# Six loads at a time, reciprocals over DRAM and whole visits in the opening of a fused attention and MLP kernel

## The chip, the cores and the metric

One core of one Trainium2 chip. Times are device microseconds of a whole execution; a ratio is taken only against runs of the kernel before in the same rounds on the same chip, because the kernel before alone reads 379 to 391 us from chip to chip and round to round. Ratios and their intervals are of fast runs alone; the medians are of all runs. With one core at work a run is called slow by its time alone, when it lies over 1.5% above the fastest run of the same kernel, so a ratio of a few runs leans on the fastest one. Pairs and visits are counted from 0: the fifth visit is V(5).

## The reference, cut to what matters

```python
# B, H, S, D = 8, 8, 576, 64; factor = 4
out_d     = softmax(q_d @ k_d.T / 8) @ v_d      # q, k, v averaged over 4 tokens
out_local = softmax(q @ k.T / 8 where |i-j| < 4) @ v
x         = (repeat(out_d, 4) + out_local)      # -> 4608 tokens x 512
h         = x @ w_in                            # 512 x 2048
out       = (h * sigmoid(h)) @ w_out            # 2048 x 512
```

## The kernel before

Attention works on 32 pairs of heads. Each pair has these units: T (transposes Q and K on TensorE), S (scores), Z (the softmax sums), PV (output), and, for the first eight pairs, VP (the averaged V by matmul). The MLP has 144 first-layer groups of 4 matmuls and 36 x 4 second-layer groups of 4. A small planner in the kernel orders all units on each engine; the order is then fixed. Up to pair 9 the units stand one by one (the prologue); from there a *visit* V(n) holds PV of pair n-2, Z of pair n-1, S of pair n and T of pair n+1 in one block, and MLP groups stand between visits.

The sums have to be inverted and spread over 64 partitions. For the first eight pairs TensorE does that, from three bf16 parts of the reciprocal; for all others the reciprocals are written to DRAM and read back as a broadcast:

```python
def after_Z(p):
    one("DVE", f"r{p}", 1.2, lambda e: e.reciprocal(zr[i], CD[:, :, 360:432]), ...)
    if p < NDIR:                       # NDIR = 8: parts for TensorE
        ... rh (ACT), rx, rm, rl (DVE)
        return
    dma("ACT", f"z{p}", scr[u], zf, ...)                # 72 KB to DRAM
    for h in range(2):
        dma("ACT", f"b{p}", Rb[u][half(h)], src, ...)   # 2 x 180 KB back, broadcast

def RB(p):                             # 18 matmuls into AB, then ACT copies AB to Rb
    ...

def after_PV(p):                       # DVE: xo = CD * Rb, then POOL adds into xT
    ...

        T(0)
        for n in range(10):
            T(n + 1); S(n)
            if n > 0: Z(n - 1)
            if n > 1: PV(n - 2)
            if 0 < n <= NDIR:
                RB(n - 1); VP(n - 1)
            if n > 4: G1((2, 4, 4, 4, 2)[n - 5])
        for n in range(10, 46):
            V(n); ...                  # with 4 first-layer and 4 second-layer groups
```

(Cut: constants, loads, casts, the planner.) CD, two of the eight PSUM banks, takes the sums of one pair and the output of another; pairs 1 and 3 use HP instead, which the MLP's first layer needs as well. Loads of Q, K and V are issued by SP, weights by POOL.

The softmax here doesn't subtract the row's maximum and nothing guards it: scores larger than these inputs give would overflow.

## Time and profile before

The median is 382.89 us of three runs (379.94 to 384.25); in the rounds with the changed kernel 383.57 of four. The profiled execution has a span of 378.6 us. Two stretches tell it: up to the tenth visit, and the rest (columns: length, busy us and count of TensorE, weight loads, DVE, ACT and POOL, granted clock, DMA share, GB/s).

```profile
0.00:92.17 92.17, 61.00 (x1505) 46.44 (x1506) 62.13 (x119) 45.46 (x91) 60.62 (x96) 0.98 1.04 249
92.17:378.60 286.43, 277.05 (x3842) 174.81 (x3872) 175.60 (x260) 131.43 (x229) 108.01 (x119) 0.99 0.52 145
```

TensorE idles 31.2 of 92.2 us in the prologue and 9.4 of 286.4 us afterwards. So most of what can be won lies in the prologue.

### The profile page before, as it was taken

The numbers are of one execution on the slowest core, as the hardware profiler recorded it, in microseconds if no ns is written. First come the engines' busy times: TensorE is split into PE (matmuls) and PEld (weight loads), VectorE is DVE, ScalarE is ACT, GpSimd is POOL, SyncE is SP. The second block draws the span as 40 slices with busy tenths as digits, with TensorE's granted clock in tenths as the row PEclk, the third lists the DMA queues.
The fourth block names the chain that finished last, engine by engine and source line by source line (L and its number), as shares of the span: only waits on it lengthen the run. The fifth ranks groups of instructions, "written<-read, shape, count | busy, mean of one in ns | idle before, by whom it ended". The sixth has DMA issues, their size and how long they took to land.

```text
span 378.6 us, 12323 instructions
## 1 busy us (share of the span) xinstructions
PE 338.1 (89%) x5346; PEld 221.3 (58%) x5376; DVE 237.7 (63%) x379; ACT 176.9 (47%) x320; POOL 168.6 (45%) x215
## 2 busy tenths in 40 slices
PE   2475689886999989989999999999999999999996
PEld 1364576654566656656665666666656566666642
DVE  6555468698677858877787776778875434434310
ACT  3635356554355535545544545555543343443421
POOL 6849568367455736665655566555221100000000
PEclk9999999899999999999999999999999999999999
DMA  7999999958978896887887887522222211001012
GB/s 211 280 290 308 244 275 244 237 161 232 257 174 245 220 271 164 222 242 212 223 219 214 213 225 214 162 96 79 84 77 79 66 39 44 28 31 54 28 57 83
DMA packets 77823, 64.37 MB, mean 170 GB/s; under 512 B 47050, under 2 KB 59850, under 8 KB 77770
## 3 DMA queue, kind: packets, MB, share of 16 engines
q1 hardware_dynamic: 66250, 46.68, 45.3%
q10 hardware_dynamic: 7296, 10.62, 10.4%
q0 software_dynamic: 4224, 6.29, 7.7%
q8 instruction: 42, 0.69, 0.8%
q14 instruction: 11, 0.09, 0.1%
HBM read 54.46 MB, written 11.21 MB: 173 GB/s over the span
## 4 chain that ended last, share of the span: by engine, by line
PE 77%; DMA 8%; DVE 4%; SPq 4%; issue 4%; ACT 2%; ACTq 1%; POOL 0%; POOLq 0%
PE HP L339 35%; PE o L339 22%; PE pe_ L339 7%; DMA scr<-zr 6%; PE CD L339 6%; PE AB L339 4%; SPq L426 4%; DMA qk<-in_k_dram 2%; PE o L531 1%; ACTq L426 1%; PE pe_ L531 1%; DVE Pt L586 1%; DVE gT L773 1%; DVE xo L728 1%; DVE gT L699 1%
## 5 line engine op out<-in xcount | busy, mean ns | idle before, releaser
L339 PE MATMUL HP<-xT,w_in_sb 128*128 128x512 f32 x576 | 164.1, 421 | 2.4 <-DVE gT L773 2.4
L773 DVE SCALAR_TENSOR_TENSOR gT<-th,HP 128x512 bf16<-128x512 f32 x144 | 96.4, 683 | 96.9 <-ACT th L771 96.9
L771 ACT ACTIVATE th<-HP 128x512 f32<-128x512 f32 x144 | 85.8, 598 | 84.1 <-PE HP L339 80.5
L339 PEld LDWEIGHTS HP<-xT,w_in_sb 128*128 128x128 f32 x576 | 106.8, 191 | 29.6 <-DVE gT L773 3.1
L339 PE MATMUL o<-w_out_bf,gT 128*128 128x512 bf16 x437 | 102.0, 380 | 1.8
L339 PEld LDWEIGHTS o<-w_out_bf,gT 128*128 128x128 bf16 x464 | 42.1, 98 | 56.1 <-issue 5.7
L755 POOL TENSOR_TENSOR xT<-xo 128x576 fp32r<-128x576 f32 (+3 forms) x48 | 44.4, 938 | 62.7 <-DVE xo L728 62.7
L513 POOL CAST vb<-vs 128x640 bf16<-128x640 f32 x30 | 21.5, 717 | 60.6 <-PE CD L339 52.5
L788 ACT ACTIVATE osb<-o 128x512 f32<-128x512 f32 x29 | 17.3, 597 | 60.9 <-PE o L339 49.7
L690 DVE RECIPROCAL zr<-CD 128x144 f32<-128x144 f32 x30 | 31.7, 1056 | 9.9 <-PE CD L339 5.2
L503 POOL CAST qkb<-qk 128x1152 bf16<-128x1152 f32 x30 | 34.6, 1154 | 3.6 <-PE pe_ L531 2.9
L518 POOL TENSOR_TENSOR vt<-vq 128x512 f32<-128x512 f32 x24 | 30.6, 1274 | 0.2 <-POOL vd L520 0.2
L728 DVE TENSOR_TENSOR xo<-CD,Rb 128x720 f32<-128x720 f32 x30 | 26.8, 895 | 0.0
L339 PE MATMUL pe_<-w_out_bf,gT 128*128 128x512 bf16 x109 | 26.1, 380 | 0.2
L531 PE MATMUL o<-idn,qkb 64*64 64x64 bf16 x576 | 17.6, 206 | 8.8 <-DVE qkb L498 5.6
L545 DVE TENSOR_REDUCE kd<-kT 128x144 bf16<-128x576 bf16 x32 | 23.6, 737 | 0.7 <-ACT kT L541 0.6
L541 ACT ACTIVATE kT<-pe_ 128x576 bf16<-128x576 bf16 x32 | 20.9, 652 | 6.7 <-PE pe_ L531 6.2
L582 ACT ACTIVATE Pt<-AB 128x576 bf16<-128x576 f32 x32 | 20.7, 647 | 6.1 <-PE AB L339 3.8
L531 PEld LDWEIGHTS o<-idn,qkb 64*64 64x64 bf16 x576 | 14.2, 119 | 11.7 <-DVE qkb L498 6.5
L531 PE MATMUL pe_<-idn,qkb 64*64 64x64 bf16 x576 | 17.1, 206 | 1.3 <-DVE qkb L500 0.7
L339 PE MATMUL CD<-Pd,vd 64*64 64x72 bf16 x360 | 15.1, 210 | 3.3 <-DVE xo L728 3.0
L339 PEld LDWEIGHTS pe_<-w_out_bf,gT 128*128 128x128 bf16 x112 | 10.0, 98 | 13.6 <-issue 3.2
(78 smaller groups left out, 350.9 us busy)
## 6 DMA issues: line engine op xcount, KB each, us to landing
vs<-in_v_dram SPq DMA_DIRECT2D x126, 80.0 KB, 4.1
qk<-in_q_dram SPq DMA_DIRECT2D x32, 288.0 KB, 4.9
out_dram<-osb SPq DMA_DIRECT2D x36, 256.0 KB, 2.1
qk<-in_k_dram SPq DMA_DIRECT2D x31, 288.0 KB, 5.7
Rb<-scr ACTq DMA_DIRECT2D x48, 180.0 KB, 4.7
vq<-in_v_dram SPq DMA_DIRECT2D x24, 256.0 KB, 5.9
w_in_sb<-in_moe_w_in_dram POOLq DMA_DIRECT2D x4, 1024.0 KB, 9.9
w_out_bf<-in_moe_w_out_dram POOLq DMA_DIRECT2D x4, 512.0 KB, 8.2
```

The lines of the kernel that those rows point to most:

```text
L339: L.op(u, lambda t: t.matmul(out_, lhsT, rhs, start=start, stop=stop, skip_group_check=True), r, w)
L503: one("POOL", f"c{p}", 1.15, lambda g: g.tensor_copy(qkb[j][:, :, :], qk[i][:, :, :]), r=[R(f"qk{i}0"), R(f"qk{i}1")], w=[R(f"qkb{j}0"), R ...
L513: one("POOL", f"cw{p}", 0.72, lambda g: g.tensor_copy(vb[m][:, :, :], vs[i][:, :, :]), r=rr, w=[R(f"vb{m}")])
L518: one("POOL", f"va{p}", 1.3, lambda g: g.tensor_tensor(vt[:, :, :], vq[i][:, :, 0:128], vq[i][:, :, 128:256], ALU.add), r=rr, w=[R("vt")])
L531: L.op(u, lambda e, o=o, w=w, j=j: e.transpose(o, w, idn[half(j), :]), [R("id"), R(f"qkb{n}{x}")], [rE if x else rF])
L541: one("ACT", f"ek{p}", 0.68, lambda e: e.activation(kT[j][:, 3:579].rearrange("p (g r) -> p g r", r=9), pe_[:, 0:288].bitcast(BF16).rearra ...
L545: one("DVE", f"mk{p}", 0.74, lambda e: e.tensor_reduce(kd[j][:, 0:SD], kT[j][:, 3:579].rearrange("p (g r) -> p g r", r=4), AX.X, ALU.add), ...
L690: one("DVE", f"r{p}", 1.2, lambda e: e.reciprocal(zr[i][:, :, :], CD[:, :, 360:432]), r=rCD, w=[R(f"zr{i}")], prio=-4)
L728: one("DVE", f"m{p}", 0.92, lambda e: e.tensor_tensor(xo[x][:, :, :].rearrange("p x (m n) -> p x m n", n=72), CD[:, :, 0:360].rearrange("p ...
L755: one("POOL", f"a{p}", 0.15 + n * 0.0019, lambda g, dst=dst, in0=in0, in1=in1: g.tensor_tensor(dst, in0, in1, ALU.add), r=[R(f"xo{x}")], w ...
L771: one("ACT", f"t{j}_{f}", 0.62, lambda e: e.activation(th[tb][:, :], hps[hb], AF.Tanh, scale=0.5), r=[rH[hb]], w=[R(f"th{tb}")], prio=-1)
L773: one("DVE", f"s{j}_{f}", 0.71, lambda e: e.scalar_tensor_tensor(gT[j % 2][:, f, :], th[tb][:, :], 1.0, hps[hb], ALU.add, ALU.mult), r=[rH ...
```

## The change

Its intent: hold the loads of later pairs back so that the next pair's arrive soon; take the broadcasts off TensorE in favour of a round trip over DRAM (except pair 3); and use whole visits from V(5) on. Weights are also asked for later, priorities are strengthened, and the query sums of pairs 4 to 7 go from POOL to DVE.

```diff
-NDIR = 8
+DIRECT = (3,)
+NFLOW = 6
@@ a load takes one of six tokens, and waits for the landing of the load that had it @@
+            if flow:
+                x = R(f"flow{nflow[0] % NFLOW}")
+                nflow[0] += 1
+                r, w = list(r) + [x], list(w) + [x]
@@ after_T @@
-            if p >= NVP:
+            if p >= 4:
                 one("DVE", f"mq{p}", ...)
@@ after_Z @@
-            if p < NDIR:
+            if p in DIRECT:
@@ weights @@
-        for c, t in enumerate((10, 14, 18, 22, 34, 38, 42, 46)):
+        for c, t in enumerate((16, 23, 29, 35, 41, 46, 51, 56)):
             load_w(c).ready = float(t)
@@ the prologue @@
-        for n in range(10):
+        for n in range(5):
             T(n + 1); S(n); Z(n - 1); VP(n - 1); PV(n - 2)      # shortened
-                RB(n - 1)
+        RB(3)
+        PV(3)
+        G1(3)
+        V(5)
+        G1(3)
+        for n, m in zip(range(6, 10), (3, 3, 2, 2)):
+            VP(n - 2)
+            V(n)
+            G1(m)
```

(Cut: priorities, the issue of the first K loads from ACT, the rule that a pair's V is not asked for before its Q and K, and the main loop, whose contents stay.)

More of the change, by code (lines that the diff above doesn't have):

```diff
@@ L167, in __init__ @@
         self.units = []
+        self.boost = 0
     def unit(self, eng, name, cost, prio=None, dcost=0.0):
@@ L172, in unit @@
         if u.prio is None:
-            u.prio = u.idx
+            u.prio = u.idx - self.boost
         self.units.append(u)
@@ L421, in constants, with dma @@
                     base=-64 * j, pattern=[[-1, 5], [0, 64]], channel_multiplier=1), r=selr, w=selr)
-        def dma(eng, name, out_, in_, w, sem, dcost, r=(), prio=None, cost=0.42):
+        nflow = [0]
+        def dma(eng, name, out_, in_, w, sem, dcost, r=(), prio=None, cost=0.42, flow=False):
+            if flow:
+                x = R(f"flow{nflow[0] % NFLOW}")
+                nflow[0] += 1
+                r, w = list(r) + [x], list(w) + [x]
             return one(eng, name, cost, lambda s: s.dma_start(out_, in_), r, w, sem, prio, dcost)
@@ L429, in load_qk @@
             i = p % NQK
+            ek = "ACT" if p < 2 else "SP"
             if p == 0:
-                dma("SP", "lkx", Rb[NR - 1][64:128, 0:576], bass.AP(tensor=k.tensor, offset=k.offset,
+                dma("ACT", "lkx", Rb[NR - 1][64:128, 0:576], bass.AP(tensor=k.tensor, offset=k.offset,
                                                                    ap=[[576, 64], [1, 576]]),
-                    [R(f"Rb{NR - 1}1")], "kx", 0.5, prio=-20)
+                    [R(f"Rb{NR - 1}1")], "kx", 0.5, prio=-20, flow=True)
             dma("SP", f"lq{p}", qk[i][:, 0, :], bass.AP(tensor=q.tensor, offset=q.offset + 128 * p * 576,
                                                         ap=[[576, 128], [1, 576]]),
-                [R(f"qk{i}0")], f"qk{i}0", 0.85, prio=10 * p)
+                [R(f"qk{i}0")], f"qk{i}0", 0.85, prio=10 * p, flow=True)
             n = 128 if p < NPAIR - 1 else 64
-            dma("SP", f"lk{p}", qk[i][0:n, 1, :], bass.AP(tensor=k.tensor, offset=k.offset + (128 * p + 64) * 576,
+            dma(ek, f"lk{p}", qk[i][0:n, 1, :], bass.AP(tensor=k.tensor, offset=k.offset + (128 * p + 64) * 576,
                                                           ap=[[576, n], [1, 576]]),
-                [R(f"qk{i}1")], f"qk{i}1", 0.85, prio=10 * p)
+                [R(f"qk{i}1")], f"qk{i}1", 0.85, prio=10 * p, flow=True)
         def load_v(p):
@@ L462, in load_v @@
                                   ap=[[64, 64], [58 * 64, hi - lo], [1, 64]])
-                    dma("SP", f"lv{p}", d[:, lo:hi, :], win, w, f"vs{i}{h}{j}", 0.46, prio=10 * p + 15)
+                    dma("SP", f"lv{p}", d[:, lo:hi, :], win, w, f"vs{i}{h}{j}", 0.46, prio=10 * p + 15, flow=True)
         def load_vq(p):
@@ L471, in load_vq @@
                 bass.AP(tensor=t, offset=o, ap=[[256, 128], [S_ * D_, 2], [1, 256]]),
-                [R(f"vqm{i}")], f"vq{i}", 1.0, prio=10 * p + 21)
+                [R(f"vqm{i}")], f"vq{i}", 1.0, prio=10 * p + 21, flow=True)
             for j in range(2):
@@ L475, in load_vq @@
                     bass.AP(tensor=t, offset=o + 128 * 256, ap=[[256, 16], [S_ * D_, 2], [1, 256]]),
-                    [R(f"vqe{i}{j}")], f"vqe{i}{j}", 0.12, r=[R(f"vqc{i}1"), R(f"vqc{i}3")], prio=10 * p + 21)
+                    [R(f"vqe{i}{j}")], f"vqe{i}{j}", 0.12, r=[R(f"vqc{i}1"), R(f"vqc{i}3")], prio=10 * p + 21, flow=True)
         def load_w(c):
@@ L690, in after_Z @@
             one("DVE", f"r{p}", 1.2, lambda e: e.reciprocal(zr[i][:, :, :], CD[:, :, 360:432]),
-                r=rCD, w=[R(f"zr{i}")], prio=-4)
+                r=rCD, w=[R(f"zr{i}")], prio=-400000)
             zf = zr[i][:, :, :].rearrange("p x n -> p (x n)")
-            if p < NDIR:
+            if p in DIRECT:
                 h, m, l = rpart
-                one("ACT", f"rh{p}", 0.25, lambda e: e.activation(h, zf, AF.Copy), r=[R(f"zr{i}")], w=[rpr[0]], prio=-4)
+                one("ACT", f"rh{p}", 0.25, lambda e: e.activation(h, zf, AF.Copy), r=[R(f"zr{i}")], w=[rpr[0]], prio=-400000)
                 one("DVE", f"rx{p}", 0.22, lambda e: e.tensor_tensor(rrest, zf, h, ALU.subtract),
-                    r=[R(f"zr{i}"), rpr[0]], w=[R("g1_5")], prio=-4)
-                one("DVE", f"rm{p}", 0.16, lambda e: e.tensor_copy(m, rrest), r=[R("g1_5")], w=[rpr[1]], prio=-4)
+                    r=[R(f"zr{i}"), rpr[0]], w=[R("g1_5")], prio=-400000)
+                one("DVE", f"rm{p}", 0.16, lambda e: e.tensor_copy(m, rrest), r=[R("g1_5")], w=[rpr[1]], prio=-400000)
                 one("DVE", f"rl{p}", 0.22, lambda e: e.tensor_tensor(l, rrest, m, ALU.subtract),
-                    r=[R("g1_5"), rpr[1]], w=[rpr[2]], prio=-4)
+                    r=[R("g1_5"), rpr[1]], w=[rpr[2]], prio=-400000)
                 return
             eng = "ACT"
-            dma(eng, f"z{p}", scr[u][:, :], zf, [R(f"scr{u}")], f"scr{u}", 0.2, r=[R(f"zr{i}")], prio=-5)
+            dma(eng, f"z{p}", scr[u][:, :], zf, [R(f"scr{u}")], f"scr{u}", 0.2, r=[R(f"zr{i}")], prio=-500000)
             for h in range(2):
@@ L706, in after_Z @@
                 dma(eng, f"b{p}", Rb[u][half(h), :], src, [R(f"Rb{u}{h}")], f"Rb{u}{h}", 0.85,
-                    r=[R(f"scr{u}")], prio=-5)
+                    r=[R(f"scr{u}")], prio=-500000)
         def RB(p):
@@ L755, in after_PV @@
                 one("POOL", f"a{p}", 0.15 + n * 0.0019, lambda g, dst=dst, in0=in0, in1=in1: g.tensor_tensor(
-                    dst, in0, in1, ALU.add), r=[R(f"xo{x}")], w=xblk(kc, t + a, t + e_), prio=-2)
+                    dst, in0, in1, ALU.add), r=[R(f"xo{x}")], w=xblk(kc, t + a, t + e_), prio=-200000)
         ng1 = [0]
@@ L824, in V @@
         def V(n):
-            pv = n - 2 if n - 2 < NPAIR else None
+            pv = n - 2 if n - 2 < NPAIR and ("PV", n - 2) not in made else None
             z = n - 1 if n - 1 < NPAIR else None
@@ L860, in feed @@
                         continue
+                    if name in ("lv", "lvq") and ("lqk", p) not in made:
+                        continue
                     made.add((name, p))
@@ L866, in bass_hourglass_attn__then__act_silu_kernel @@
         feed()
-        for c, t in enumerate((10, 14, 18, 22, 34, 38, 42, 46)):
+        for c, t in enumerate((16, 23, 29, 35, 41, 46, 51, 56)):
             load_w(c).ready = float(t)
         todo = [(j, f) for j in range(NSUP) for f in range(16)]
+        todo2 = [(j, tt) for j in range(NSUP) for tt in range(4)]
         def G1(n):
@@ L874, in G1, with G2 @@
                     g1(*todo.pop(0))
+        def G2(parts):
+            j, tt = todo2[0]
+            u = 4 * j + tt
+            bank, rb = (o0, rF) if u < 22 or u % 2 else (pe_, rE)
+            for p in parts:
+                g2(j, tt, p, bank, rb)
+            if parts[-1] == 3:
+                todo2.pop(0)
+        L.boost = 100000
         T(0)
         feed()
-        for n in range(10):
+        for n in range(5):
             T(n + 1)
@@ L883, in bass_hourglass_attn__then__act_silu_kernel @@
                 Z(n - 1)
+                VP(n - 1)
             if n > 1:
@@ L886, in bass_hourglass_attn__then__act_silu_kernel @@
                 feed()
-            if 0 < n <= NDIR:
-                RB(n - 1)
-                VP(n - 1)
-            if n > 4:
-                G1((2, 4, 4, 4, 2)[n - 5])
-        for n in range(10, 46):
+        RB(3)
+        PV(3)
+        feed()
+        G1(3)
+        V(5)
+        feed()
+        G1(3)
+        for n, m in zip(range(6, 10), (3, 3, 2, 2)):
+            L.boost = 100000 if n < 8 else 0
+            VP(n - 2)
+            V(n)
+            feed()
+            G1(m)
+        L.boost = 0
+        n = 10
+        while todo or todo2:
             if n < NPAIR + 2:
@@ L895, in bass_hourglass_attn__then__act_silu_kernel @@
                 feed()
-            j, tt = divmod(n - 10, 4)
-            bank, rb = (o0, rF) if n < NPAIR or n % 2 else (pe_, rE)
-            G1(1)
-            g2(j, tt, 0, bank, rb)
-            G1(1)
-            g2(j, tt, 1, bank, rb)
-            G1(1)
-            g2(j, tt, 2, bank, rb)
-            g2(j, tt, 3, bank, rb)
-            G1(1)
+            m = 4
+            G1(1 if m else 0)
+            G2((0,))
+            G1(1 if m else 0)
+            G2((1,))
+            G1(1 if m else 0)
+            G2((2, 3))
+            G1(m - 3 if m else 0)
+            n += 1
         P = Prog()
```

## The prediction

> **What bounds the kernel now.** I read the busy table first, then five stretches of time that I cut where the kernel changes character, then the waits of the first 92 us, then the chain that ended last around the end of that stretch.
>
> ```profile
> span 378.6 us, 12323 instructions
> PE 338.1 (89%) x5346; PEld 221.3 (58%) x5376; DVE 237.7 (63%) x379; ACT 176.9 (47%) x320; POOL 168.6 (45%) x215
> ```
>
> TensorE is the bound on average, but that average hides two kernels in one. The stretches (columns: busy us and count of PE, weight loads, DVE, ACT, POOL, then granted clock, DMA share, GB/s):
>
> ```profile
> 0.00:20.00 20.00, 7.04 (x242) 5.63 (x243) 12.17 (x45) 9.44 (x17) 14.20 (x43) 1.00 0.89 248
> 20.00:55.00 35.00, 23.45 (x646) 19.36 (x644) 19.87 (x29) 15.69 (x34) 22.10 (x28) 1.00 1.23 275
> 55.00:92.00 37.00, 30.51 (x623) 21.43 (x620) 29.98 (x47) 20.33 (x40) 24.32 (x26) 0.95 0.93 224
> 92.00:300.00 208.00, 202.04 (x3510) 130.96 (x3535) 151.63 (x226) 102.93 (x182) 108.01 (x119) 0.99 0.67 183
> 300.00:379.00 79.00, 75.02 (x333) 43.86 (x337) 24.08 (x35) 28.50 (x48) 0.00 (x0) 1.00 0.12 44
> ```
>
> From 92 us on TensorE is 97% busy (202.04 of 208) and 95% at the end; nothing there can be won without removing matmuls. Before 92 us it is busy 7.04 + 23.45 + 30.51 = 61.0 us and idle 31.0 us. That prologue is pairs 0 to 9 of attention plus the first 16 of 144 first-layer groups of the MLP, and 16 of them is also what the changed prologue holds. At 92.17 us the tenth visit starts, the first that is followed by second-layer matmuls. From there to the end the kernel takes 378.6 - 92.2 = 286.4 us.
>
> What fills the prologue's holes, from its waits and its groups:
>
> ```profile
> ACT Rb L718 <- PE AB L339: 14.5, 8, 4.7
> POOL vb L513 <- DMA vs<-in_v_dram: 8.1, 3, 3.3
> ```
>
> ```profile
> L339 PE MATMUL AB<-gT 128*128 128x144 bf16 (+1 forms) x144 | 13.1, 260 | 3.2 <-DVE gT L699 3.1
> L718 ACT ACTIVATE Rb<-AB 128x720 f32<-128x720 f32 x8 | 6.2, 771 | 14.5 <-PE AB L339 14.5
> ```
>
> The first pair: the broadcast of the reciprocals on TensorE (18 matmuls a pair, 144 in all) costs 13.1 us of TensorE, and it sits in the one in-order stream behind a split of the reciprocal in three bf16 parts on DVE and ACT. The second: the cast of V on POOL stands 8.1 us in three waits for loads. The loads behind them take a median of 8.7 us, 12.3 at most, between 15 and 40 us (17 V loads), where 275 GB/s move at a DMA share of 1.23; the first loads of the kernel land after 3 to 4 us.
>
> **What the Trainium skill says.** "DMA: Bandwidth & Descriptors", section "Queues, rings and completion order": each DMA engine goes round the queue rows that have work, packet by packet, and the SP and the ACT issuer each own a row. So fewer loads under way on SP do not lift total bandwidth; they shorten the line that a load stands in, and a transfer issued from ACT never stood in that line, it only shares the engines. The trace agrees as far as it goes: loads got slow as soon as the weight row was active. The same page, "Anatomy of one DMA", gives a fixed part of about 2 us a transfer, which is why a round trip over DRAM of two transfers cannot be short; here the trace has 2.6 to 5.2 us for the write of the reciprocals and 3.8 to 6.9 (median 5.2) for the broadcast read. "TensorE: Matmul & The Clock Gate", section "Part 1: The HAM clock gate", has half clock after some 3.4 us of idleness; the trace shows the same 18 broadcast matmuls in 1.98 us before 50 us and 0.96 us after 60, so a prologue with holes pays twice.
>
> **The change part by part.** The visits' contents after pair 9 are the same, so I ask when the tenth visit can start.
>
> Removed: seven of eight broadcasts. TensorE loses 7/8 of 13.1 = 11.5 us (some 1 us each late, 2 early), ACT 7 x 0.77 = 5.4 us, and 7 x 0.32 for the first part; DVE loses 7 x (0.37 + 0.60 + 0.70) = 11.7 us, in a prologue where DVE was 9.7 us busy of the 10 between 80 and 90. DVE gets back four query sums from POOL, 4 x 0.74 = 3.0 us.
>
> Added: seven round trips over DRAM. Each is reciprocal 1.06, issue about 0.4, landing 3 to 4.5, two issues 1.1, landing 4.7 to 7, multiply 0.90, handoffs 0.5: 12 to 15 us, with the visit's own 1.4 us. In DMA: 72 KB written and read again as 2 x 180 KB, 0.43 MB a pair, 3.0 MB in all; at 275 GB/s that is 11 us of DMA time. The accumulator banks couple it to TensorE: from the fifth visit on visit n+2 may not write before the multiply of visit n's reciprocals, because both live in the same PSUM banks. So two interleaved chains, odd and even visits, each step 12 to 15 us long, that is a visit every 6 to 7.5 us. The matmul work of such a visit is 1.3 (visit) + 0.9 (V sums) + 2 x 0.9 (two first-layer groups) = 4 us, so the round trip, not TensorE, sets the pace there.
>
> The start, worked through the changed order of instructions with durations of the trace. Until 12 us nothing changes: the first scores wait for constants on POOL (the before trace has them at 11.5). Then the second pair's scores come forward, the third pair's come at about 19.5 instead of 22.3, because no broadcast stands before them (2 us) and its V load is not behind six others. The first pair's reciprocal is ready at 17.3, written by 21 to 22, broadcast by 27 to 29, multiplied by 29. The third Z needs that bank, so it stands at 29 to 30 (before: 29.3; nothing won yet). Then scores of pair 4, PV of pair 2, V sums, about 34; the multiply of pair 1 (its broadcast is behind ACT's evacuations, 35 to 36) frees the other bank; Z, PV and the one remaining broadcast of pair 3 end at about 41; the multiply of pair 2 lands at 43 to 45. The fifth visit starts at about 44. (Before, the comparable work, S5 and Z4, was at 47 to 51.)
>
> From there: visit 7 at 44 + 12 to 15 = 56 to 59, visit 9 at 68 to 74. The even chain starts later, since the first two first-layer groups need the first four pairs multiplied and added (47.5) and are in front: visit 6 at 50.5, visit 8 at 62.5 to 65.5, visit 10 at 75 to 80. I take 80, the slow end, because loads, weights and broadcasts share the DMA there. A check on bytes: by then 12 pairs of Q and K (6.9 MB), 9 of V (2.9), two of the V means (0.6), the weights (6.3 as the queue counts them) and the round trips (3.0) must have come, 19.7 MB, and prefetch adds some 2: 22 MB in 76 us is 285 GB/s, against 308 as the best 10 us of the trace. So DMA just carries it and cannot carry much more.
>
> Sum: the tenth visit at 80 instead of 92.2, minus 12.2; one first-layer group is left for after it, plus 0.9; net 11.3 us. Of the 31 us of idle time about 11.5 us go with the removed TensorE work; the rest stays as waits of another name. 382.9 - 11.3 = 371.6; I write 371.
>
> **The rivals.** (a) The round trip is hidden and DMA is not in the way: two chains at 12 us and short loads put the tenth visit at 74 or 75; minus 17, about 366. For it: in the steady part the round trip of 13 us is fully hidden at 8.7 us a visit. Against: less work per visit here. (b) DMA becomes the bound: the loads held to six fall to under 200 GB/s or the broadcasts take 8 us beside weights; the tenth visit starts at 87 to 90 and the time is 378 to 381. For it: the share was 1.23 in 20 to 55 us, and 3 MB are added. Against: weights are asked for later (the second-layer ones by POOL after the ninth pair's casts), and loads for pairs 12 to 14 no longer run ahead. (c) The limit of six starves the steady part. A visit has nine loads; 2 x 5.3 + 4 x 4.1 + 5.9 + 2 x 5.3 = 43.5 us of landing time (medians of the page) over six lanes is 7.3 us, under the 8.7 of a visit, so it is just hidden; if landings rise by a fifth it is not, and 20 visits at 0.5 us would take 10 us back: 381. (d) TensorE goes cold in waits of 4 us or more between visits 6 to 10, some 1 us a visit: plus 4, at 375.
>
> **Range and chances.** The middle is 371. Rival (a) sets the low end at 363, (b) or (c) the high end at 380. The 2% line is 375.2, that is a tenth visit at about 84; my two chains would have to be 2 us a step slower than their slow end. I give 0.74 to faster, 0.23 to the same, 0.03 to slower, since even rival (c) in full only gives back the gain.
>
> **What would show it.** Right: 18 matmuls from gT into AB instead of 144; first second-layer matmul before 85 us (before: 96.8) and a span from there to the end as before within 2 us; TensorE idle in front of CD matmuls, released by DVE's multiply, in 50 to 80 us, and the chain there running over DMA to scr and Rb; V loads landing under 6 us in 15 to 40 us. Wrong: second-layer matmuls starting after 92 us; POOL casts waiting for loads in the steady part and a visit of more than 8.8 us; or, on the good side, no wait for the multiply at all.

## The result, and the profile after

The changed kernel is slower: 397.08 us median (395.01 to 398.12, four runs) against 383.57, ratio 1.038 (95% interval 1.028 to 1.047). A ratio here is the mean time of one kernel's fast runs over that of the other's of the same rounds, so not quite the ratio of the medians.

The page's first lines and the same two stretches, cut at the changed kernel's tenth visit:

```profile
span 392.9 us, 12068 instructions
PE 332.1 (85%) x5220; PEld 214.7 (55%) x5250; DVE 231.6 (59%) x362; ACT 169.1 (43%) x306; POOL 162.7 (41%) x207
```

```profile
0.00:101.83 101.83, 53.96 (x1374) 39.99 (x1374) 53.01 (x99) 36.59 (x74) 51.92 (x85) 0.93 0.99 233
101.83:392.90 291.07, 278.09 (x3846) 174.74 (x3876) 178.54 (x264) 132.55 (x232) 110.82 (x122) 1.00 0.54 150
```

Up to the tenth visit every engine has less to do (TensorE 7.0 us less), and yet TensorE idles 47.9 us there where it idled 31.2. Of the 14.3 us of span, 9.7 come before the tenth visit and 4.6 after it; 0.9 of the latter is the first-layer group that the change leaves for later, as predicted.

The chain of work that ended last, followed back from the last instruction, shows where the time went (shares of the span, the kernel before and then the changed one):

```profile
PE 77%; DMA 8%; DVE 4%; SPq 4%; issue 4%; ACT 2%; ACTq 1%; POOL 0%; POOLq 0%
```

```profile
PE 57%; DMA 34%; SPq 4%; issue 1%; DVE 1%; ACT 1%; ACTq 1%; POOL 0%; POOLq 0%
```

In the changed kernel 31 of the 34% of DMA are loads of V (13%), K (10%) and the averages of V (8%); the writes of the reciprocals have 3%. Such a chain names one path only; a second one that ends almost as late does not show in it, which is why the runs below are needed.

What the idle time waits for. These are waits of the first 110 us (engine, line, what it waited for: us in total, times, longest):

```profile
POOL vb L522 <- DMA vs<-in_v_dram: 22.1, 6, 6.2
DVE xo L737 <- DMA Rb<-scr: 13.6, 5, 4.9
PE CD L341 <- DVE xo L737: 12.1, 6, 5.1
POOL vt L527 <- DMA vq<-in_v_dram: 10.6, 3, 5.8
```

Two new families. The multiply on DVE waits for the broadcast from DRAM, and TensorE waits for that multiply before it may write CD again. And POOL's casts wait for V loads 22.1 us, where it was 8.1. The issuing queue of SP shows the limit; first the two longest waits of the kernel before, then those of the changed one, in the first 110 us:

```profile
SPq L426 <- POOL vt L518: 5.5, 1, 5.5
SPq L426 <- POOL qd L558: 1.8, 1, 1.8
```

```profile
SPq L434 <- DMA vs<-in_v_dram: 26.2, 15, 4.3
SPq L434 <- DMA qk<-in_k_dram: 10.1, 11, 1.4
SPq L434 <- DMA qk<-in_q_dram: 3.6, 5, 1.7
SPq L434 <- DMA vq<-in_v_dram: 2.0, 3, 1.5
```

Before, the queue only waited for free buffers. Now it stands 41.9 us until some load has landed.

One round trip, that of pair 4, can be followed through the timelines of DVE, ACT and TensorE of the changed kernel (start, length, what; in brackets the idle time before it and what ended it):

```profile
54.87 1.06 DVE L699 RECIPROCAL zr<-CD 128x144 f32<-128x144 f32 x1 [0.86 <-PE CD L341]
...
70.42 0.91 DVE L737 TENSOR_TENSOR xo<-CD,Rb 128x720 f32<-128x720 f32 x1 [3.92 <-DMA Rb<-scr]
```

```profile
55.96 0.33 ACTq L434 DMA_DIRECT2D scr<-zr  x1
...
61.26 1.28 ACTq L434 DMA_DIRECT2D Rb<-scr  x2
```

```profile
71.38 0.28 PE L341 MATMUL CD<-Pd,vd 64*64 64x72 bf16 x4 [5.14 <-DVE xo L737]
```

The reciprocal is done at 55.9, and its write is issued at once. The broadcast can be issued at 61.3 only, when the write has landed (5.2 us), and the multiply starts at 70.4, 9.2 us after that. The seventh visit, whose first matmuls are the TensorE line above, begins right behind it. From the end of the sums (54.7) to the end of the multiply (71.3) the trip took 16.6 us. The same measure, read along each engine's order, gives 16.6, 17.5 and 20.6 us for pairs 5 to 7, and 14.6, 20.5 and 19.5 for pairs 0 to 2.

Pair 7's 20.6 us are not landings alone. ACT issues the broadcasts in its own order, so its next activation stands behind an issue that waits for a landing. Here it is pair 6's broadcast that waits, until 82.3 us; the activation behind it, whose matmuls had ended at 79.7, starts at 83.5, a product on DVE waits for that activation, and pair 7's reciprocal, whose sums had ended at 81.3, for that product:

```profile
82.34 1.10 ACTq L434 DMA_DIRECT2D Rb<-scr  x2
83.49 0.60 ACT L780 ACTIVATE th<-HP 128x512 f32<-128x512 f32 x1 [6.21 <-issue]
```

```profile
84.12 0.69 DVE L782 SCALAR_TENSOR_TENSOR gT<-th,HP 128x512 bf16<-128x512 f32 x1 [3.56 <-ACT th L780]
84.72 1.05 DVE L699 RECIPROCAL zr<-CD 128x144 f32<-128x144 f32 x1
```

So one trip's landing cost the next trip 3.4 us: the chains of odd and even visits are not independent.

### The profile page after: what moved, and what is told of

Read it like the earlier page. It is cut to its first block, busy times and chain, and to the rows that moved or that the text cites. A ratio compares the mean times of both kernels' runs of the same rounds, so it can differ in the third digit from the quotient of the medians.

```text
span 392.9 us, 12068 instructions
## 1 busy us (share of the span) xinstructions
PE 332.1 (85%) x5220; PEld 214.7 (55%) x5250; DVE 231.6 (59%) x362; ACT 169.1 (43%) x306; POOL 162.7 (41%) x207
## 4 chain that ended last, share of the span: by engine, by line
PE 57%; DMA 34%; SPq 4%; issue 1%; DVE 1%; ACT 1%; ACTq 1%; POOL 0%; POOLq 0%
PE HP L341 25%; PE o L341 20%; DMA vs<-in_v_dram 13%; DMA qk<-in_k_dram 10%; DMA vq<-in_v_dram 8%; PE pe_ L341 6%; SPq L434 4%; PE CD L341 3%; DMA scr<-zr 3%; PE AB L341 1%; ACTq L434 1%; PE pe_ L540 1%; ACT osb L797 1%; PE o L540 1%; DVE gT L782 1%
## 5 line engine op out<-in xcount | busy, mean ns | idle before, releaser
L341 PE MATMUL HP<-xT,w_in_sb 128*128 128x512 f32 x576 | 166.5, 427 | 13.0 <-DVE gT L782 11.6
L341 PEld LDWEIGHTS HP<-xT,w_in_sb 128*128 128x128 f32 x576 | 108.3, 194 | 44.7 <-DVE gT L782 12.2
L764 POOL TENSOR_TENSOR xT<-xo 128x576 fp32r<-128x576 f32 (+3 forms) x48 | 43.6, 922 | 48.2 <-DVE xo L737 48.2
L558 DVE TENSOR_REDUCE qd<-qT 128x144 bf16<-128x576 bf16 x28 | 20.8, 743 | 1.7 <-ACT qT L344 1.7
L595 DVE TENSOR_TENSOR Pt<-Pt,mask_bf 128x576 bf16<-128x576 bf16 x32 | 18.2, 568 | 3.5 <-ACT Pt L591 3.5
```

Of the source, the lines that this page charges most:

```text
L341: L.op(u, lambda t: t.matmul(out_, lhsT, rhs, start=start, stop=stop, skip_group_check=True), r, w)
L764: one("POOL", f"a{p}", 0.15 + n * 0.0019, lambda g, dst=dst, in0=in0, in1=in1: g.tensor_tensor(dst, in0, in1, ALU.add), r=[R(f"xo{x}")], w ...
```

## The experiments

Theory A, formed from these views: the limit starves the casts. Theory B: the round trips are long and the banks that they hold stop TensorE. Theory C: whole visits, late weights and priorities are to blame. The table sums up the runs. "Fifth visit" is its start, and in kernels without whole visits (in brackets) the start of Z of pair 4, its first part. "Second layer" is the first instruction of the second layer on TensorE (a weight load); from there to the end the correct kernels' fast profiles take 281 to 288 us.

| run | what it is | median us | ratio to before | 95% interval | fifth visit | second layer |
|---|---|---|---|---|---|---|
| before | | 382.89 | 1 | | (47.4) | 96.8 |
| changed | limit, trips, visits | 397.08 | 1.038 | 1.028-1.047 | 53.3 | 107.0 |
| e1 | changed, no waits of the limit | 395.80 | 1.040 | 1.025-1.054 | 50.6 | 107.4 |
| e2 | changed, no trips | 391.33 | 1.027 | 1.013-1.041 | 43.5 | 106.5 |
| e3 | changed, no limit, no trips | 385.26 | 1.005 | 1.001-1.008 | 40.8 | 99.5 |
| e4 | before + limit | 386.99 | 1.012 | 1.000-1.024 | (47.6) | 97.6 |
| e5 | before + trips | 389.60 | 1.014 | 1.007-1.021 | (53.0) | 104.3 |
| e6 | changed, a quarter of the weights' bytes (wrong result) | 387.45 | 1.010 | 1.001-1.019 | 47.6 | 93.9 |
| e7 | changed, trips for pairs 0-2 only | 398.86 | 1.040 | 1.032-1.048 | 54.1 | 114.7 |
| e8 | before + query sums of pairs 0, 1 on DVE | 380.57 | 0.988 | 0.981-0.994 | (44.8) | 92.0 |
| e9 | changed, trips for pairs 4-7 only | 393.92 | 1.021 | 1.015-1.026 | 44.9 | 103.1 |
| e10 | before + query sums of pairs 0-7 on DVE | 385.37 | 0.989 | 0.981-0.996 | (47.2) | 93.5 |
| e11 | before + query sums of pairs 0-3 on DVE | 384.96 | 0.998 | 0.994-1.002 | (48.7) | 96.5 |
| e12 | e8 again | 380.54 | 0.986 | 0.982-0.989 | | |

At the 2% line the recorded verdicts are slower for the changed kernel, same for e3, e8, e10, e11 and e12, and unclear for the others; below, the intervals are argued from. The medians of e9 to e11 stand beside 385.6 of the kernel before in their rounds, those of e5 to e8 beside 384.5, those of e1 to e4 beside 384.4, that of e12 beside 385.5. The profiles of e10 and e12 fell in the slow state; no time is read from them except the two marks of e10, which lie before any second-layer work and are given for completeness.

**e1, the limit's waits taken out, order kept.**

```diff
-                P.op(u.eng, fn, r, w, d)
+                P.op(u.eng, fn, [x for x in r if x.name[:4] != "flow"],
+                     [x for x in w if x.name[:4] != "flow"], d)
```

The tokens guard no data, so nothing races without them. The planner has run by then, so every engine keeps its order, one that was planned with the limit.

> The changed kernel, every engine's order of instructions kept, with only the waits of the limit of six taken out. Theory A (the limit starves the casts: the queue of SP stood 42 us in waits for landings in the first 110 us, and six loads that land after 9 us are too low a rate): the queue no longer waits for landings, the first second-layer matmul moves from 107 us to 85 to 97, the time falls to 375 to 386. Theory B (the seven round trips over DRAM and the bank that they hold): at most 3 us better, 393 or more. Theory C (late weights and whole visits): 393 or more as well.

Measured: 395.8 us. Theory A in this form fell. Waits of the first 105 us:

```profile
PE CD L341 <- DVE xo L737: 17.2, 6, 5.6
DVE xo L737 <- DMA Rb<-scr: 17.0, 5, 6.0
POOL vb L522 <- DMA vs<-in_v_dram: 9.7, 2, 8.7
```

The casts' waits halve (22.1 to 9.7), and the waits for round trips take the place (12.1 to 17.2). In the chain that ended last the writes of the reciprocals now take 16% of the span and the loads of V 1%, where it was 3% and 13%, and the time is the same. That fits two paths that end about equally late: taking one out gains nothing.

The run also tests what the limit was for. Landing times of the V loads issued in 20 to 55 us, in the kernel before (23 loads), the changed one (16) and e1 (19):

```profile
DMA to landing us min/median/max: 5.8/8.2/12.3
```

```profile
DMA to landing us min/median/max: 3.5/9.0/12.5
```

```profile
DMA to landing us min/median/max: 3.3/8.2/14.4
```

Beside the trips, fewer loads under way did not land sooner (9.0 us with the limit, 8.2 without). The same view of the runs without early trips, which follow below, says otherwise: e4, the kernel before with the limit (16 loads), e2 with the limit (19) and e3 without it (23):

```profile
DMA to landing us min/median/max: 2.9/6.2/10.7
```

```profile
DMA to landing us min/median/max: 4.5/6.9/7.8
```

```profile
DMA to landing us min/median/max: 5.4/8.6/11.0
```

There the limit shortens a landing: 6.2 us against 8.2 in the kernel before, 6.9 against 8.6 in e3. So the limit shortens landings as meant until the trips are added. These times start at the issue, so what a load waits for its token is not in them, and in each comparison fewer loads are issued in the stretch with the limit.

**e2, the limit kept, reciprocals of the first eight pairs on TensorE.**

```diff
-DIRECT = (3,)
+DIRECT = tuple(range(8))
                 Z(n - 1)
+                RB(n - 1)
                 VP(n - 1)
-        RB(3)
         PV(3)
             VP(n - 2)
+            RB(n - 2)
             V(n)
```

> The changed kernel with the limit of six kept, but the reciprocals of the first eight pairs broadcast on TensorE as before. Theory A: loads are as slow as before, 390 or more. Theory B: no multiply waits for a transfer and 3 MB less move, 376 to 385. Theory C: 390 or more.

Measured: 391.3 us, within A's and C's 390 or more, and outside B's band. The fifth visit comes 9.8 us earlier than in the changed kernel, and the tenth at 92.7. But the second layer starts only at 106.5. The waits of the first 105 us show why:

```profile
POOL vt L527 <- DMA vq<-in_v_dram: 18.0, 3, 10.1
...
PE HP L341 <- POOL xT L764: 10.7, 2, 7.5
```

POOL stands before the averages of V, its load being late, and the additions into xT behind them hold the first layer up on TensorE. That the limit is what costs here, once the trips no longer hide it, the next run shows.

**e3, neither limit nor trips.** The edit of e2, and:

```diff
-NFLOW = 6
+NFLOW = 400
```

> The changed kernel without the limit and with the broadcasts on TensorE; what is left of the change is whole visits, the later weights and the new priorities. A and B: about the time of the kernel before, 376 to 386. C: 390 or more.

Measured: 385.3 us, ratio 1.005 (1.001 to 1.008). Theory C fell: whole visits, late weights, priorities and the smaller parts of the change together cost half a per cent. Against e2 the second layer starts 7.0 us earlier and the time is 6.1 us less, which is what the limit costs in this form. (The planner saw other waits here than in e2, so parts of the early order differ as well.)

**e4, the limit alone on the kernel before.**

```diff
+            if eng == "SP" and name[0] == "l" and name[-1] != "e":
+                x = R(f"flow{nflow[0] % 6}")
+                nflow[0] += 1
+                r, w = list(r) + [x], list(w) + [x]
@@ feed @@
+                    if name in ("lv", "lvq") and ("lqk", p) not in made:
+                        continue
```

> The kernel before with the limit of six alone (and the rule that a pair's V is not asked for ahead of its Q and K, without which the limit would order them badly). A: 390 or more, the queue of SP waiting for landings for 30 us or more before the first second-layer matmul. B and C: 380 to 387.

Measured: 387.0 us, ratio 1.012 with an interval that just touches 1. A's 390 is missed, and so are its 30 us of waits (SP stood 25.5 us in the first 105); the band of B and C is held at its edge. A small cost is likely, not shown.

**e5, the trips alone on the kernel before.**

```diff
-            if p < NDIR:
+            if p in (3,):
-                RB(n - 1)
+                if n - 1 == 3:
+                    RB(n - 1)
                 VP(n - 1)
```

> The kernel before with one part of the change alone: reciprocals over DRAM for the first eight pairs except the fourth; no limit, no whole visits, early weights. After the first four runs theory B is: a round trip takes 17 to 20 us from the last matmul of the sums to the end of the multiply wherever other transfers are under way, and the banks that it holds stop TensorE. B: 390 to 396. Rival D (a trip costs that much only where visits are whole, because a whole visit writes the sums of one pair and the output of another into the same banks): 381 to 386.

Measured: 389.6 us, ratio 1.014, just under B's band and above D's. Rival D fell: without whole visits the trips of pairs 4 to 7 take as long (16.6, 19.8, 17.2, 18.1 us), and Z of pair 4 starts 5.6 us later than before. But the price is 1.4% here, and 3.5% between e3 and e1 (1.040 over 1.005), so whole visits may make the trips dearer without making them longer. That is argued, not shown: e1 and e3 also differ in the order that was planned, and no run tests this part by itself.

**e6, a quarter of the weights' bytes, wrong on purpose.**

```diff
-            load_w(c).ready = float(t)
+            if c % 4 == 0:
+                load_w(c).ready = float(t)
@@ g1 and g2 take chunk 0 for all four chunks @@
```

> The changed kernel with only the first quarter of each weight matrix loaded and used for all four: wrong results on purpose, the same matmuls, 1.6 MB on the weights' queue instead of 6.3. If the trips are long because weights and loads share the DMA engines with them: trips of pairs 4 to 7 fall from 17 to 20 us to 13 to 15, the tenth visit comes before 90 us and the time is 376 to 385. If a trip is long by itself or by the order on ACT: trips stay at 16 us and more and the time stays at 391 or more.

Measured: trips of pairs 4 to 7 take 16.2, 14.0, 12.2 and 15.7 us, a mean of 14.5 against 17.8 in the changed kernel; the tenth visit starts at 89.0; the time is 387.5 (two runs), 2.5 us above the band. Landing times of the trips' transfers issued in 45 to 105 us, first in the changed kernel (15 transfers), then here (19):

```profile
DMA to landing us min/median/max: 3.4/6.5/8.3
```

```profile
DMA to landing us min/median/max: 2.8/5.2/9.2
```

So without three quarters of the weights' bytes a trip is 3.3 us shorter, and the stretch from the fifth to the tenth visit takes 41.4 us instead of 48.6. (The median of transfers includes the steady part's first; a landing that has no end in the records is left out of it.) Fewer bytes also help the loads, so the whole gain of the time is not the trips'.

**e7, pairs 3 to 7 on TensorE, pairs 0 to 2 over DRAM,** and **e9, the reverse.**

```diff
-DIRECT = (3,)
+DIRECT = (3, 4, 5, 6, 7)      # e7, with RB(n - 2) in the visits
+DIRECT = (0, 1, 2, 3)         # e9, with RB(n - 1) in the first loop
```

> The changed kernel with its limit, pairs 0 to 2 over DRAM as there, but pairs 3 to 7 on TensorE. If the visits five to ten, which the trips of pairs 4 to 7 pace, carry the loss: the stretch from the fifth to the tenth visit falls from 48.6 us to 40 or less, and the time is 388 to 392, near the kernel with all eight on TensorE (391.3). If the first three trips carry it: 394 or more.

> The counterpart of the run with pairs 3 to 7 on TensorE: the changed kernel with its limit, pairs 0 to 3 on TensorE, pairs 4 to 7 over DRAM. If the first three trips carry what the trips cost beside the limit: 389 to 394 with a fifth visit at 45 us or earlier (53 in the changed kernel), and a time near that of all eight on TensorE (391). If the four later trips carry as much by themselves: 395 or more although the fifth visit comes early.

Measured: e7 398.9 us (fifth visit 54.1), e9 393.9 (fifth visit 44.9). Taking the four later trips out gains nothing; taking the first three out gains about 1.7% (1.021 against 1.038) although the later four stay. In e7 the stretch from the fifth to the tenth visit still lasts 48.6 us as in the changed kernel, now behind loads: in its first 105 us POOL waits 23.0 us for V and 14.1 for the averages' loads. In e9 it lasts 48.5 us.

Before the fifth visit the four kernels with and without limit and trips add up (one profile each): the trips cost 9.8 us there (53.3 against 43.5 with the limit, 50.6 against 40.8 without), the limit 2.7 (53.3 against 50.6, 43.5 against 40.8). Behind it they do not: the stretch to the tenth visit lasts 48.6 us in the changed kernel, 49.7 in e1, 49.2 in e2 and 53.5 in e3, which has neither. The way over TensorE is no shorter in that stretch: from the start of the reciprocal to the end of the multiply it takes 16.2 us on average for pairs 4 to 7 in the kernel before and 16.5 in e3, against 16.8 over DRAM in the changed kernel. For pairs 0 to 2 it is 12.6 and 9.3 against 18.0. So the early trips are a loss that these runs show, and the late ones are not; what else fills the stretch stays open, but for the weights' bytes (e6). My expectation for e7 (40 us for that stretch) was wrong; its other branch, 394 or more, held, and so did 389 to 394 with an early fifth visit for e9, just.

**e8, e10, e11, e12, a part of the change, tried on other pairs.** The change also moves query sums from POOL to DVE, for pairs 4 to 7. On POOL those of pairs 0 and 1 stand behind the constants:

```diff
-            if p >= NVP:
+            if p >= NVP or p < 2:         # e8 and e12; True in e10; p < 4 in e11
                 one("DVE", f"mq{p}", ...)
```

> Not of the theories but of a gain: the kernel before with the query sums of the first two pairs on DVE, as the change does for pairs 4 to 7, because on POOL they stand behind the constants until 10.2 us. The first scores end at about 10 us instead of 11.7; if that carries through, 1 to 2 us less than before, 0.995 to 1.0; if the later loads set the pace, no difference.

> The kernel before with the query sums of all first eight pairs on DVE (the change has it for pairs 4 to 7, the last gain run had it for 0 and 1). If POOL's in-order wait for V loads in front of the sums holds up the scores: 0.98 to 0.985 of before. If DVE, 8 times 0.74 us busier in the prologue, takes it back: 0.99 to 1.0.

> The same for pairs 0 to 3 alone, where DVE has room and POOL waits for loads: 0.98 to 0.988 if the wait on POOL is what matters, no better than 0.988 if only the constants in front of pair 0 and 1 mattered.

> The same kernel as the gain run with the query sums of pairs 0 and 1 on DVE, once more, because its two relatives (all eight pairs 0.9885, four pairs 0.998) do not line up with its 0.988. If the gain is real: 0.98 to 0.994 again. If it was the draw of that chip: 0.995 to 1.003, and then no version here is called better than the kernel before.

Measured: 0.988 and, again, 0.986 for pairs 0 and 1; 0.989 for all eight, between its two bands; 0.998 for the first four. The 0.989 rests on three fast runs of six; the medians of all runs are 385.4 and 385.6, so for all eight no gain is shown. The sums of the first two pairs (the instructions that write qd in the first 20 us: counts, then min/median/max ns, first and last start), before and in e8:

```profile
L558 POOL TENSOR_TENSOR qd<-vt x2: 424/424/425, 10.9 to 15.3; 128x144 bf16<-128x144 f32 x2
```

```profile
L549 DVE TENSOR_REDUCE qd<-qT x2: 746/750/753, 9.4 to 11.6; 128x144 bf16<-128x576 bf16 x2
```

The second pair's sum starts 3.7 us earlier, and the second layer 4.8 us earlier. The gain of 4 to 5 us is more than the 1 to 2 I had expected, and the weaker result with four pairs does not fit a simple account: the planner makes another order for each. The version for pairs 0 and 1 is faster than the kernel before by 1.2% and 1.4% in two sets of runs on two chips (1.0% and 1.3% by the medians of all runs), clear of noise though under the 2% line; which part of its new order brings the rest is open.

## Why the prediction was wrong

The direction was wrong: 371 us predicted, 397 measured. The predicted span was 367.3 us, the measured one 392.9, and the missing 25.6 us split along my own steps: 9.3 before the fifth visit, 12.6 from the fifth to the tenth, 3.7 after it.

**Removed work: right, and worth little.** TensorE is 7.0 us less busy before the tenth visit, where I had 11.5 us of work removed and did not count what else moved; DVE 9.1 us less and ACT 8.9. Some of the broadcasts had stood on the chain that ended last in the kernel before (1.91 us at 27.0, for one), but in the changed kernel landings stand in their place.

**"The fifth visit starts at about 44": this step failed, in the landing times of the first three trips.** I had the multiplies of pairs 0, 1 and 2 end by 29, 36 and 43 to 45 us; they ended at 32.2, 40.6 and 53.2. Pair 1's write was issued 2.7 us late, behind pair 0's broadcast in ACT's order, and landed after 9.4 us, pair 2's after 7.5, where I had 3 to 4.5. The fifth visit came at 53.3. e2, e3 and e9, which have no early trips, start it at 43.5, 40.8 and 44.9, so what I had as the time with the trips is about the time without them, and e9 against the changed kernel shows that these three trips decide a good part of the loss.

**"Each step 12 to 15 us long": the wait was right, the term mis-sized, and it was not the only bound.** Every visit from the seventh to the tenth starts right behind the multiply that frees CD, as the prediction named. But the steps measured 18.1 and 19.5 us (visits 5, 7, 9) and 18.4 and 21.8 (visits 6, 8, 10). My own parts of a step add up to 11.7 to 15.5 us, and to 13.1 to 16.9 with the visit's own 1.4, so the sum was short from the start. The landings that I took were those of the steady part of the kernel before: 3 to 4.5 for the write and 4.7 to 7 us for the broadcast, where pairs 4 to 7 had 5.2 to 7.8 for the write and pair 4 had 9.2 from the issue of the broadcast to the multiply. The steady part moves 209 to 223 GB/s at a share of 0.80 to 0.84, the prologue runs at shares up to 1.2 beside the weights, and in e6 a trip is 3.3 us shorter without most of the weights. I had noted the higher share, and still took times from the lower one. Pair 7 lost 3.4 us more behind pair 6's landing in ACT's and DVE's order, so my two chains were not independent. And I had 36 us for the stretch; e2 and e3, with no trips in it, take 49.2 and 53.5, so better landing times alone would not have made that number right. What sets the stretch without trips stays open.

**"Fewer loads under way shorten the line that a load stands in": right without the trips, wrong beside them.** I expected V loads to land under 6 us in 15 to 40 us. With the limit and no early trips they did (medians of 5.8 in e4 and 5.6 in e2); in the changed kernel the median was 8.6, as in the kernel before (8.7). What I left out is that the loads land later where the trips are added: with the trips alone (e5) the median in that stretch was 12.1 us, though 8.6 in 20 to 55 us. At a landing of 9 us six tokens are too few: SP stood 41.9 us waiting for landings. I had put the danger in the steady part, with landings of 4 to 6 us (rival c), not in the prologue, where the trace of the kernel before already had 8.7. By itself the limit costs about 6 us where no early trip ends later (e2 against e3; in e4 a cost is likely only), and nothing measurable beside the trips (e1).

**Rival (b), which made DMA the bound, was nearest** (378 to 381), and still too kind. It would have needed the tenth visit at 87 to 90; it came at 101.8. Yet DMA moved less up to there than in the kernel before (233 GB/s at a share of 0.99, against 249 at 1.04), which speaks for single transfers that landed late, one after another, and not for a lack of throughput.

**The tail** lost 3.7 us beyond the planned 0.9. POOL waits there 19.3 us for loads of V's averages, which would be rival (c), but e1, without the limit, has no such waits and loses 6.3 us there. This stays open.

**Two readings of the trace were off**, with no weight in the sum. The 18 broadcast matmuls take 1.12 us after 60 us in the timeline that gives 1.98 before 50; the 0.96 is the piece of them that stands in the chain that ended last. And the writes of the reciprocals in the steady part took 2.3 to 5.2 us up to 240 us, not 2.6 to 5.2.

## What to carry to other kernels

Take the duration of a transfer from a stretch with the same traffic as the one it will run in; a round trip that is hidden at 8.7 us a visit says nothing about one beside a weight load. A limit on loads under way can shorten their landing (8.2 to 6.2 us here) and still cost time, and its gain can go when other transfers are added (9.0 us beside the trips); check the landings and the waits together. And when several waits run side by side, taking one out, or relieving the busiest engine, moves nothing until the one that ends last has gone.

## What the Trainium skill lacked or had wrong

- "DMA: Bandwidth & Descriptors", section "Queues, rings and completion order", describes the round among queue rows, but gives no size for what a small transfer pays beside busy rows. Here a write of 72 KB from ACT landed after 5.2 to 7.8 us for pairs 4 to 7, beside 2.3 to 5.2 in the steady part up to 240 us, and a trip was 3.3 us shorter without three quarters of the weights' bytes.
- The same page, "Anatomy of one DMA", has a fixed part of about 2 us, for the path through POOL alone; the page has no such fit for transfers issued from ACT. Here a chain of a write and a broadcast read from ACT took 14.6 to 20.6 us from the sums to the end of the multiply in the prologue.
- No page says what a limit on loads under way does to their landing. Here, for V loads in 20 to 55 us: 6.2 us with six against 8.2 without it (e4, the kernel before), 6.9 against 8.6 (e2, e3), but 9.0 against 8.2 beside the trips (the changed kernel, e1).
- "TensorE: Matmul & The Clock Gate", section "Part 1: The HAM clock gate", was not contradicted: the same 18 matmuls, where nothing broke them up, took 1.98 us up to 50 us and 1.12 after 60. The granted clock of the profiles could not be read for this in the opening: it shows 1.00 for the kernel before in 20 to 55 us, where three of its broadcasts take 1.98 us of TensorE or more, and 0.66 for e8, whose broadcasts at 27 and 38 us take 1.98 as well; the first clock record of the kernel before stands at 52.1 us.
